# Two heads' keys per load, and the softmax's cross-partition steps on TensorE: a one-token decode block on one core

## The chip, the cores and the metric

The kernel runs on one core of a Trainium2 chip. The metric is device time in microseconds. The time before is 685.73 us, the median of 3 runs (685.69 to 685.84). The profile comes from a run of its own.

## The reference

One token passes through a transformer block: attention over a cache of 16,384 positions with 32 heads of 128 (each with keys and values of its own), then a gated feed-forward part. Six vectors from a condition `c` shift, scale and gate both parts.

```python
mod = (silu(c) @ w_mod).reshape(1, 6, 1, 640)        # sa, ca, ga, sb, cb, gb
h = layernorm(x) * (1 + ca) + sa
q = (h @ wq).reshape(32 heads, 128)
p = softmax(q . k_cache * 128 ** -0.5)               # 32 x 16384
o = p @ v_cache
x = x + ga * (o.reshape(4096) @ wo)
h = layernorm(x) * (1 + cb) + sb
x = x + gb * ((silu(h @ w_gate) * (h @ w_up)) @ w_down)
```

All tensors are bf16. Keys and values are 134.2 MB each; the weights together are 22.0 MB. Every byte is read once.

## The kernel before, in words

`build` writes a list of operations, each with an engine, a position (`pos`) and the operations that it depends on. `_Plan.emit` sorts each engine's operations by position and puts semaphore waits ahead of an operation whose dependencies are on other engines. So every engine runs a fixed order, and one that waits holds up all that stands behind it. All large loads go through SP's queue in such an order. `TK(h)` is the position at which head h's work begins.

**Start.** SP loads `w_mod` into `wreg`, `wq` into the space of the values (`vbig`), and then the keys of head 0 in four pieces and those of head 1. TensorE makes two of the six modulation vectors (`o_mod`, L330), and from them the normalised input. Eight groups of four heads (`q_ops`, L352) give the queries, broadcast to all partitions, and ScalarE copies them to `qbc` (L356). The other four modulation vectors (`o_mod_b`) come after all eight groups.

**Keys.** A head's keys lie as 128 partitions with 128 positions each, 32,768 contiguous bytes per partition (`kv`). `kring` has two such slots. VectorE multiplies the slot by the query (L434), folds the 128 products of each position to 64 (L436), to 32 and 16 (L443), and reduces these (L446) to the scores `S_sb`; L449 takes the largest per partition. The slot is then free, and SP loads the keys of the head after the next (`load_k`).

**Softmax.** GpSimd's `partition_all_reduce` takes the maximum over the partitions (L452). ScalarE scales it (L454) and makes the exponentials `P_sb` with their sum per partition (L456); GpSimd adds the sums over the partitions (L459), and ScalarE inverts them (L461, L463).

**Values.** `vring` has two slots as well, partitions and positions as the keys have them. TensorE multiplies four columns of `P_sb` with 512 columns of values, 32 times a head (L472), so the diagonal of a 4 x 4 grid of blocks holds the wanted sums. ScalarE copies the four rows out with the scaling (L484), and four small matmuls add the diagonal (L491). The value slot is free when L472's last matmul is done (`o_pvlast`); SP loads the values of the head after the next then (`load_v`). In TensorE's order, head h's product stands at `TK(h) + 28.0`, before the work of the following heads.

**End.** Heads 0 to 27 are turned to columns in groups (L515, L519), heads 28 to 31 are used as they are. The last head's values come in three pieces, each used as it lands, in matmuls of one column (L502). `wo` lies in `wreg`, and its matmuls (L560) collect the attention's output. The feed-forward weights are loaded into `kring` once the last two heads' scores are made. Then follow the second layer norm, gate and up (L624), down (L642), the sum with x (L648), a transpose and the output's store.

Of the kernel before, what the change touches and what calls it, by code (L numbers as in the profile page):

```python
# [6 lines left out]
BF16 = mybir.dt.bfloat16  # L7
# [134 lines left out]
def build(nc, A_x, A_k, A_v, A_wq, A_wo, B_wg, B_wu, B_wd, c_in, w_mod, out):  # L142
# [10 lines left out]
    GQ = 4  # L153
    PVB = 4
# [7 lines left out]
    NKP0 = 4  # L162

    def TK(h):
        return 20.0 + PERIOD * h

    es = ExitStack()
    with es:
# [3 lines left out]
        def sb(name, shape, dtype):  # L172
# [7 lines left out]
        VEX = 10240  # L180
        wreg = sb("wreg", [128, max(WM_E, H * D)], BF16)
        wm_v = wreg[:, 0:WM_E].rearrange("p (k n) -> p k n", k=KC)
        wo_v = wreg[:, 0:H * D].rearrange("p (k n) -> p k n", k=H)
        kring = sb("kring", [128, 2, TT, 128], BF16)
        vbig = sb("vbig", [128, 2 * TT * 128 + VEX], BF16)
        vring = vbig[:, 0:2 * TT * 128].rearrange("p (s t d) -> p s t d", s=2, t=TT)
        assert WQ_E - VEX <= TT * 128
        wq_v = vbig[:, 2 * TT * 128 + VEX - WQ_E:2 * TT * 128 + VEX].rearrange("p (k n) -> p k n", k=KC)
        assert FFN_E <= 2 * TT * 128
        kflat = kring[:].rearrange("p s t d -> p (s t d)")  # L190
        wg_v = kflat[:, 0:KC * F].rearrange("p (k n) -> p k n", k=KC)
        wu_v = kflat[:, KC * F:2 * KC * F].rearrange("p (k n) -> p k n", k=KC)
        wd_v = kflat[:, 2 * KC * F:2 * KC * F + FCH * D].rearrange("p (k n) -> p k n", k=FCH)
        acc_sb = sb("acc_sb", [4, 2, 512], F32)
        ident_f = sb("ident_f", [4, 4], F32)
        qbc = sb("qbc", [128, H, 128], BF16)
        S_sb = sb("S_sb", [128, 2, TT], F32)
        P_sb = sb("P_sb", [128, 2, TT], BF16)
        ones_f = sb("ones_f", [128, 128], F32)
# [10 lines left out]
        c_one = acc_sb[0:1, 0].bitcast(BF16)[:, 0:D]  # L210
        x_one = acc_sb[0:1, 1].bitcast(BF16)[:, 0:D]
        pm = sb("pm", [128, H], F32)
        gm = sb("gm", [128, H], F32)
        nb = sb("nb", [128, H], F32)
        rs = sb("rs", [128, H], F32)
        Ls = sb("Ls", [128, H], F32)
# [3 lines left out]
        warm = sb("warm", [128, 2], F32)  # L220
# [31 lines left out]
        mod_ps = psb[4]  # L252
        A_ps = psb[5]
        st_ps = psb[6]
        f_ps = psb[7]
        acc_ps = [psb[0], psb[1]]
# [3 lines left out]
        POOL, ACT, DVE, PE = "pool", "act", "dve", "pe"  # L260
# [4 lines left out]
        o_ones = op(POOL, 0.0, lambda e: e.memset(ones_bf[:], 1.0), name="ones")  # L265
        o_ident = op(POOL, 0.1, lambda e: e.affine_select(
            out=ident[:], in_=ones_bf[:], pattern=[[1, 128]], compare_op=ALU.is_equal,
            fill=0.0, base=0, channel_multiplier=-1), deps=[o_ones], name="ident")
        o_wz = op(DVE, 0.1, lambda e: e.memset(warm[:], 1.0), name="warm0")
        op(POOL, 0.2, lambda e: e.partition_all_reduce(  # L270
            warm[:, 1:2], warm[:, 0:1], channels=128, reduce_op=bass.bass_isa.ReduceOp.max), deps=[o_wz], name="warm")
# [72 lines left out]
        def q_ops(pos, g, wv, n0, ddep, h0, h1):  # L344
            n = h1 - h0
            b = g % 2
            prev = o_qev.get(g - 2)

            def f_q(e):
                last = None  # L350
                for k in range(KC):
                    last = e.matmul(q_ps[b][:, 0:n * 128], lhsT=h_col[:, k:k + 1].broadcast_to([128, 128]),  # L352
                                    rhs=wv[:, k, n0:n0 + n * 128], start=(k == 0), stop=(k == KC - 1))
                return last
            o_q[g] = op(PE, pos, f_q, deps=[ddep, o_h, prev], name="q_mm%d" % g)
            o_qev[g] = op(ACT, pos + 0.1, lambda e: e.activation(  # L356
                out=qbc[:, h0:h1].rearrange("p h d -> p (h d)"), in_=q_ps[b][:, 0:n * 128], func=ACTF.Copy),
                deps=[o_q[g]], name="qbc%d" % g)
            for h in range(h0, h1):
                o_qbc[h] = o_qev[g]  # L360

        o_qbc = [None] * H
# [5 lines left out]
        o_mod_b = op(PE, 4.5, lambda e: f_mod(e, wm_v, 2, 6, lambda o, k: slice(o + 128 * k, o + 128 * (k + 1))), deps=[d_wm, o_h], name="mod_mm_b")  # L368
        o_modc = op(ACT, 4.6, lambda e: e.activation(out=modb[:], in_=mod_ps[:, 2 * KC:6 * KC], func=ACTF.Copy), deps=[o_mod_b], name="mod_b")
        o_onep_b = op(DVE, TK(0) + 19.3, lambda e: e.tensor_scalar_add(out=onep_b[:], in0=modb[:, 2 * KC:3 * KC], scalar1=1.0), deps=[o_modc], name="onep_b")  # L370
        ga, sb_, gb = modb[:, 0:KC], modb[:, KC:2 * KC], modb[:, 3 * KC:4 * KC]
        o_gbx = op(DVE, TK(0) + 19.35, lambda e: e.tensor_copy(out=gbx, in_=gb), deps=[o_modc], name="gb_pairs")
# [3 lines left out]
        d_k = [None] * H  # L376
        d_v = [None] * H
        o_red = [None] * H
        o_exp = [None] * H
        o_pvlast = [None] * H  # L380
        o_acc = [None] * H
        o_diag = [None] * H
        o_on = [None] * H
        o_z = [None] * H
        TL = TK(H - 1)
        VSPLIT = [0, TT // 2, 3 * TT // 4, TT]

        def load_k(h):
            s2 = h % 2
            deps = [o_red[h - 2]] if h >= 2 else []  # L390
            if h == 0:
                KP = TT // NKP0
                d_k[0] = [plan.dma(0.2 + 0.01 * c, kring[:, 0, c * KP:(c + 1) * KP, :], kv(A_k, 0)[:, c * KP:(c + 1) * KP, :],
                                   ("k0", c), name="dma_k0_%d" % c) for c in range(NKP0)]
                return
            d_k[h] = [plan.dma(TK(h - 1) + 8.8 if h > 1 else 0.3, kring[:, s2], kv(A_k, h), ("k", s2), deps=deps, name="dma_k%d" % h)]

        def load_v(h, pos):
            s2 = h % 2
            cuts = VSPLIT if h == H - 1 else [0, TT]  # L400
            deps = [o_pvlast[h - 2]] if h >= 2 else o_q_all
            d_v[h] = [plan.dma(pos + 0.01 * c, vring[:, s2, a:b, :], kv(A_v, h)[:, a:b, :],
                               ("v", s2, c), deps=deps, name="dma_v%d_%d" % (h, c)) for c, (a, b) in enumerate(zip(cuts, cuts[1:]))]

        load_k(0)
        load_k(1)

        o_idf = op(ACT, 4.7, lambda e: e.activation(out=ident_f[:], in_=ident[0:4, 0:4], func=ACTF.Copy), deps=[o_ident], name="ident_f")
        o_msk, o_e8 = {}, {}
        for n in msk:  # L410
            o_msk[n] = op(DVE, TK(0) + 19.0, lambda e, n=n: e.tensor_reduce(  # L411
# [5 lines left out]
            o_e8[n] = op(DVE, TK(0) + 19.05, f_e8, deps=[o_ident], name="e%d" % n)  # L417
        o_as = [None] * len(GROUPS)

        for h in range(H):  # L420
            base = TK(h)
            s2 = h % 2
            if h + 1 < H and h >= 1:
                load_k(h + 1)
            load_v(h, base + 8.9 + (0.5 if h == H - 1 else 0.0))

            kslot = kring[:, s2]
            npc = len(d_k[h])
            KP = TT // npc
            fd = []  # L430
            for c in range(npc):
                ksl = kslot[:, c * KP:(c + 1) * KP, :]
                qb = qbc[:, h].unsqueeze(1).broadcast_to([128, KP, 128])
                o_m = op(DVE, base + 3.3 * c, lambda e, ksl=ksl, qb=qb: e.tensor_tensor(out=ksl, in0=ksl, in1=qb, op=ALU.mult),  # L434
                         deps=[d_k[h][c], o_qbc[h]], name="mult%d_%d" % (h, c))
                fd.append(op(DVE, base + 3.3 * c + 2.2 + (6.6 if npc == 1 else 0.0), lambda e, ksl=ksl: e.tensor_tensor(  # L436
                    out=ksl[:, :, 0:64], in0=ksl[:, :, 0:64], in1=ksl[:, :, 64:128], op=ALU.add),
                    deps=[o_m], name="fold1_%d_%d" % (h, c)))
            prev = fd
            w = 64  # L440
            for i in range(2):
                w //= 2
                prev = [op(DVE, base + 15.5 + 1.5 * i, lambda e, kslot=kslot, w=w: e.tensor_tensor(  # L443
                    out=kslot[:, :, 0:w], in0=kslot[:, :, 0:w], in1=kslot[:, :, w:2 * w], op=ALU.add),
                    deps=prev, name="fold%d_%d" % (i + 2, h))]
            o_red[h] = op(DVE, base + 18.2, lambda e, s2=s2, kslot=kslot, w=w: e.tensor_reduce(  # L446
                out=S_sb[:, s2], in_=kslot[:, :, 0:w], axis=AX.X, op=ALU.add),
                deps=prev + [o_exp[h - 2] if h >= 2 else None], name="red%d" % h)
            o_max = op(DVE, base + 18.5, lambda e, h=h, s2=s2: e.tensor_reduce(  # L449
                out=pm[:, h:h + 1], in_=S_sb[:, s2], axis=AX.X, op=ALU.max), deps=[o_red[h]], name="max%d" % h)  # L450

            o_gm = op(POOL, base + 19.0, lambda e, h=h: e.partition_all_reduce(  # L452
                gm[:, h:h + 1], pm[:, h:h + 1], channels=128, reduce_op=bass.bass_isa.ReduceOp.max), deps=[o_max], name="gm%d" % h)
# [13 lines left out]
            if h < H - 1:  # L467


                def f_pv(e, s2=s2):  # L470
# [6 lines left out]
                    with e.Fori(0, (TT - 16) // (4 * PVB)) as i:  # L477
                        for u in range(PVB):
                            one(i * (4 * PVB) + (8 + 4 * u), i * (512 * PVB) + (v0 + 1024 + 512 * u))
# [224 lines left out]
```

## Time and profile before

| | |
|---|---|
| Median of 3 runs | 685.73 us |
| Profiled run, its time | 685.91 us |
| Its span, from the first to the last instruction | 684.2 us |
| PE busy (matmul) | 354.2 us, 52% |
| DVE busy | 617.6 us, 90% |
| ACT busy | 79.6 us, 12% |
| POOL busy | 375.4 us, 55% |
| Mean granted TensorE clock | 0.729 |
| Read from memory | 290.48 MB, 425 GB/s over the span |

PE is TensorE, DVE is VectorE, ACT is ScalarE, POOL is GpSimd and SP is SyncE, which here only issues loads. A line of the profile names a line of the kernel (L434), an engine, an operation, and what it writes and reads. In a timeline each row has its start and its busy time in us, and in square brackets the idle time of the engine just before it and what ended that. The chain of waits is followed back from the last instruction, at each step to whatever released it. The shares of the DMA's time are shares of the core's 16 DMA engines.

### The profile page before, as it was taken

The numbers are of one execution on the slowest core, as the hardware profiler recorded it, in microseconds if no ns is written. First come the engines' busy times: TensorE is split into PE (matmuls) and PEld (weight loads), VectorE is DVE, ScalarE is ACT, GpSimd is POOL, SyncE is SP. The second block draws the span as 40 slices with busy tenths as digits, with TensorE's granted clock in tenths as the row PEclk, the third lists the DMA queues.
The fourth block names the chain that finished last, engine by engine and source line by source line (L and its number), as shares of the span: only waits on it lengthen the run. The fifth ranks groups of instructions, "written<-read, shape, count | busy, mean of one in ns | idle before, by whom it ended". The sixth has DMA issues, their size and how long they took to land.

```text
span 684.2 us, 6292 instructions
## 1 busy us (share of the span) xinstructions
PE 354.2 (52%) x1952; PEld 151.5 (22%) x1952; DVE 617.6 (90%) x228; ACT 79.6 (12%) x280; POOL 375.4 (55%) x71
## 2 busy tenths in 40 slices
PE   2345244556544544656554444655545446555565
PEld 2122012222211212222121212222112112221254
DVE  0299999999999999999999999999999999999911
ACT  1021011011101111111011111111011110110010
POOL 0005765655567766655567756655573666555700
PEclk9977676776777776676677777677767776777665
DMA  9999999999999999999999999999999999999996
GB/s 379 410 438 429 433 434 433 430 431 435 435 428 429 431 429 429 433 435 431 432 437 430 433 428 431 431 428 431 431 433 433 433 435 432 429 429 433 410 413 270
DMA packets 13689, 290.70 MB, mean 425 GB/s; under 512 B 1318, under 2 KB 2024, under 8 KB 4200
## 3 DMA queue, kind: packets, MB, share of 16 engines
q1 hardware_dynamic: 13668, 290.48, 99.2%
q8 instruction: 10, 0.16, 0.1%
q14 instruction: 7, 0.06, 0.0%
q10 hardware_dynamic: 4, 0.00, 0.0%
HBM read 290.48 MB, written 0.00 MB: 425 GB/s over the span
## 4 chain that ended last, share of the span: by engine, by line
DVE 79%; DMA 17%; SPq 3%; issue 1%; PE 0%; ACT 0%; DVEq 0%
DVE kring L434 35%; DVE kring L436 18%; DVE kring L443 14%; DMA kring<-in_A_k_cache_dram 12%; DVE S_sb L446 9%; DMA vbig<-in_A_wq_dram 4%; SPq L71 3%; DMA kring<-in_B_w_down_dram 2%; DVE pm L449 1%; PE psb L352 0%; PE psb L642 0%; ACT qbc L356 0%; DVE e L416 0%; DVE msk L411 0%; PE psb L652 0%
## 5 line engine op out<-in xcount | busy, mean ns | idle before, releaser
L472 PE MATMUL psb<-vbig,P_sb 128*4 128x512 bf16 (+1 forms) x992 | 285.7, 459 | 266.8 <-ACT P_sb L456 193.1
L452 POOL PARTITION_ALL_REDUCE gm<-pm x32 | 254.7, 7960 | 226.6 <-DVE pm L449 226.6
L434 DVE TENSOR_TENSOR kring<-kring,qbc 128x16384 bf16<-128x16384 bf16 (+1 forms) x35 | 278.4, 7953 | 14.6 <-ACT qbc L356 13.4
L472 PEld LDWEIGHTS psb<-vbig,P_sb 128*4 128x4 bf16 (+1 forms) x992 | 94.7, 98 | 444.7 <-ACT P_sb L456 237.2
L436 DVE TENSOR_TENSOR kring<-kring 128x8192 bf16<-128x8192 bf16 (+1 forms) x35 | 142.1, 4059 | 1.2
L459 POOL PARTITION_ALL_REDUCE Ls<-rs x32 | 119.6, 3738 | 32.7 <-ACT P_sb L456 32.7
L443 DVE TENSOR_TENSOR kring<-kring 128x4096 bf16<-128x4096 bf16 x64 | 112.5, 1758 | 2.2
L446 DVE TENSOR_REDUCE S_sb<-kring 128x128 f32<-128x2048 bf16 x32 | 73.2, 2286 | 1.1
L491 PE MATMUL psb<-ident_f,acc_sb 4*128 4x1 f32 x248 | 32.5, 248 | 23.8 <-ACT acc_sb L484 23.8
L484 ACT ACTIVATE acc_sb<-psb,rl 4x512 f32<-4x512 f32 x31 | 21.0, 679 | 165.3 <-PE psb L472 165.3
L491 PEld LDWEIGHTS psb<-ident_f,acc_sb 4*128 4x128 f32 x248 | 29.9, 186 | 39.5 <-ACT acc_sb L484 39.5
L454 ACT ACTIVATE nb<-gm 128x1 f32<-128x1 f32 x32 | 6.5, 202 | 214.3 <-POOL gm L452 214.3
L461 ACT ACTIVATE lnl<-Ls 128x1 f32<-128x1 f32 x32 | 6.5, 203 | 123.6 <-POOL Ls L459 123.6
L352 PE MATMUL psb<-vbig,h_col 128*128 128x512 bf16 x40 | 11.8, 468 | 10.7 <-DMA vbig<-in_A_wq_dram 10.7
L599 DVE TENSOR_TENSOR tt<-attn_bf,modb 128x5 f32<-128x5 bf16 x1 | 0.2, 167 | 14.3 <-ACT attn_bf L598 14.3
L456 ACT ACTIVATE P_sb<-S_sb,nb 128x128 bf16<-128x128 f32 x32 | 12.9, 402 | 1.2
L449 DVE TENSOR_REDUCE pm<-S_sb 128x1 f32<-128x128 f32 x32 | 9.2, 286 | 1.1
L515 ACT ACTIVATE Z<-msk,on_f 128x16 bf16<-128x16 f32 (+1 forms) x28 | 8.7, 310 | 0.9
L512 ACT ACTIVATE on_f<-psb 128x1 f32<-128x1 f32 x28 | 4.8, 171 | 31.8 <-PE psb L491 30.7
L352 PEld LDWEIGHTS psb<-vbig,h_col 128*128 128x128 bf16 x40 | 4.6, 117 | 17.5 <-DMA vbig<-in_A_wq_dram 10.8
L356 ACT ACTIVATE qbc<-psb 128x512 bf16<-128x512 f32 x8 | 4.8, 597 | 25.0 <-PE psb L352 25.0
L330 PE MATMUL psb<-silu_c,wreg 128*128 128x1 bf16 x150 | 4.8, 168 | 5.0 <-DMA wreg<-in_w_mod_dram 5.0
(75 smaller groups left out, 67.1 us busy)
## 6 DMA issues: line engine op xcount, KB each, us to landing
kring<-in_A_k_cache_dram SPq DMA_DIRECT2D x31, 4096.0 KB, 18.3
vbig<-in_A_v_cache_dram SPq DMA_DIRECT2D x31, 4096.0 KB, 27.4
vbig<-in_A_wq_dram SPq DMA_DIRECT2D x1, 5120.0 KB, 26.7
wreg<-in_w_mod_dram SPq DMA_DIRECT2D x1, 4800.0 KB, 14.2
kring<-in_A_k_cache_dram SPq DMA_DIRECT2D x4, 1024.0 KB, 31.7
wreg<-in_A_wo_dram SPq DMA_DIRECT2D x1, 3840.0 KB, 37.9
kring<-in_B_w_gate_dram SPq DMA_DIRECT2D x1, 2160.0 KB, 18.4
kring<-in_B_w_up_dram SPq DMA_DIRECT2D x1, 2160.0 KB, 23.4
```

The costliest lines, as they stand in the source:

```text
L71: return e.dma_start(out_ap, in_ap)
L352: last = e.matmul(q_ps[b][:, 0:n * 128], lhsT=h_col[:, k:k + 1].broadcast_to([128, 128]), rhs=wv[:, k, n0:n0 + n * 128], start=(k == 0), s ...
L434: o_m = op(DVE, base + 3.3 * c, lambda e, ksl=ksl, qb=qb: e.tensor_tensor(out=ksl, in0=ksl, in1=qb, op=ALU.mult), deps=[d_k[h][c], o_qbc[h ...
L436: fd.append(op(DVE, base + 3.3 * c + 2.2 + (6.6 if npc == 1 else 0.0), lambda e, ksl=ksl: e.tensor_tensor(out=ksl[:, :, 0:64], in0=ksl[:, ...
L443: prev = [op(DVE, base + 15.5 + 1.5 * i, lambda e, kslot=kslot, w=w: e.tensor_tensor(out=kslot[:, :, 0:w], in0=kslot[:, :, 0:w], in1=kslot ...
L446: o_red[h] = op(DVE, base + 18.2, lambda e, s2=s2, kslot=kslot, w=w: e.tensor_reduce(out=S_sb[:, s2], in_=kslot[:, :, 0:w], axis=AX.X, op= ...
L449: o_max = op(DVE, base + 18.5, lambda e, h=h, s2=s2: e.tensor_reduce(out=pm[:, h:h + 1], in_=S_sb[:, s2], axis=AX.X, op=ALU.max), deps=[o_ ...
L452: o_gm = op(POOL, base + 19.0, lambda e, h=h: e.partition_all_reduce(gm[:, h:h + 1], pm[:, h:h + 1], channels=128, reduce_op=bass.bass_isa ...
L459: o_L = op(POOL, base + 20.0, lambda e, h=h: e.partition_all_reduce(Ls[:, h:h + 1], rs[:, h:h + 1], channels=128, reduce_op=bass.bass_isa. ...
L472: return e.matmul(acc_ps[s2][0:4, :], lhsT=P_sb[:, s2, bass.ds(t, 4)], rhs=vbig[:, bass.ds(at, 512)], start=start, stop=stop)
L484: o_acc[h] = op(ACT, base + 28.6, lambda e, h=h, s2=s2: e.activation(out=acc_sb[:, s2], in_=acc_ps[s2][0:4, :], func=ACTF.Copy, scale=rl[0 ...
L491: last = e.matmul(OT_ps[:, h:h + 1], lhsT=acc_sb[:, s2, 128 * i:128 * (i + 1)], rhs=ident_f[:, i:i + 1], start=(i == 0), stop=(i == 3))
```

## The change

Keys are loaded two heads at a time. A unit is a pair of heads (units 0 to 14, heads 0 to 29) or a single one (units 15 and 16, heads 30 and 31). In a pair, partitions 0 to 63 hold one head and 64 to 127 the other, with 256 positions each, 65,536 contiguous bytes per partition. `kbig` has two slots of that size. `wreg` and the extra room for `wq` are gone: `w_mod` first lies in slot 1 of `kbig`, `wo` goes to slot 0 at the end, the feed-forward weights to slot 1, and `wq` fits in the values' slots. So pair 1's keys wait for all six modulation vectors, and `o_mod_b` moves up between the first two groups of queries.

GpSimd is not used any more. The largest score per partition is turned to a row by a matmul with the identity, VectorE takes the maximum of each half of that row (`top`), and a matmul with ones brings it back to the partitions. A pair's exponentials are in the keys' layout, and four matmuls with shifted identities (`place`) bring them to the values' layout, from which ScalarE copies them to `P_sb`. Sums over the partitions are a matmul with ones, for four heads at once. The scaling by the sums is taken from ScalarE's copy to VectorE, four heads at once. Masks and identities are made on VectorE at the start.

The first piece of a unit's mult is followed by the softmax of the unit before. Pair 0 comes in two pieces of 4 MB.

```diff
+    def BU(u):
+        return 20.0 + PERIOD * UNITS[u][0]
+    def EU(u):
+        return BU(u) + 18.6 * UNITS[u][1]
...
+        def load_k(u, pos, deps, cuts):
+            h, m = UNITS[u]
+            src = A_k[0, h:h + m].rearrange("h (p t) d -> (h p) t d", p=128 // m)
...
+        load_k(0, 0.2, [], [0, TT, T2])
+        load_k(1, 10.0, [o_mod, o_mod_b], [0, T2])
...
+        def stage_top(u, pos_dve):
+            o_T = op(PE, E + 0.1, lambda e: e.matmul(row_ps, lhsT=pm[:, u:u + 1], rhs=ident_f[:], start=True, stop=True),
...
+            o_sm = op(DVE, pos_dve, lambda e: e.tensor_reduce(
+                out=gm2[:, 0:m], in_=row_ps.rearrange("p (h k) -> p h k", h=m), axis=AX.X, op=ALU.max),
...
+            pt = max(E + 0.3, pos_dve + 0.01)
+            o_top[u] = op(PE, pt, f_top, deps=[o_sm, o_onesf], name="top_all%d" % u)
+            o_nb[u] = op(ACT, pt + 0.1, lambda e: e.activation(out=nb[:, u:u + 1], in_=top_ps, func=ACTF.Copy, scale=-SCALE),
...
+        for u, (h, m) in enumerate(UNITS):
+            cuts = [0, TT, T2] if u == 0 else [0, 64, nt]
...
+                if c == 0 and u:
+                    pt = softmax(u - 1, B + 4.0)
+                    hp, mp = UNITS[u - 1]
+                    if u - 1 < NU:
+                        value(hp, pt + 0.5)
+                        if hp % GQ == GQ - 2:
+                            sums(hp // GQ, pt + 0.6, hp - 2, GQ)
+                        value(hp + 1, pt + 0.7)
+                        if hp % GQ == GQ - 2:
+                            diag(hp // GQ, pt + 0.8, hp - 2, GQ)
+                    else:
+                        sums(H, pt + 0.4, hp - 2, 3)
...
+            if u < NU:
+                load_v(h, B + 8.0)
+                load_v(h + 1, B + 8.1 if u < NU - 1 else B + 8.2)
+                if u + 2 < NU:
+                    load_k(u + 2, E - 3.5, [o_red[u]], [0, T2])
...
+        pt = softmax(NU + 1, EU(NU + 1) + 0.2)
+        load_v(H - 2, BU(NU) + 6.0)
+        sums(H + 1, pt + 0.3, H - 1, 1)
+        value(H - 2, pt + 0.5)
+        diag(H // GQ - 1, pt + 0.8, HD, H - 1 - HD)
...
+        load_v(H - 1, BU(NU) + 6.2)
...
-        TO = TL + 9.0
+        TO = BU(NU) + 6.05
+        wo_free = [o_red[NU - 1]]
```

Here `NU` is 15, `TT` 128, `T2` 256, `H` 32, `HD` 28 and `GQ` 4; `value` is the product with a head's values and the copy of its four rows, and `diag` adds the diagonal blocks of up to four heads. `TL` is the position at which the last unit begins.

## The prediction

> **What bounds the kernel now.** First view: the page's DMA rows. A slice is 17.1 us.
>
> ```profile
> DMA  9999999999999999999999999999999999999996
> GB/s 379 410 438 429 433 434 433 430 431 435 435 428 429 431 429 429 433 435 431 432 437 430 433 428 431 431 428 431 431 433 433 433 435 432 429 429 433 410 413 270
> q1 hardware_dynamic: 13668, 290.48, 99.2%
> ```
>
> SP's queue keeps the 16 DMA engines full from 1.8 to 679.9 us; nothing idles until the weights of the last block are in. The chain of waits names DVE for 79% of the span; in order of time it shows why both are true:
>
> ```profile
> 476.45 8.61 DVE kring L434
> 485.08 4.44 DVE kring L436
> 489.54 2.30 DVE kring L443
> 495.44 20.50 DMA kring<-in_A_k_cache_dram
> 515.96 8.70 DVE kring L434
> ...
> 612.77 19.74 DMA kring<-in_A_k_cache_dram
> 632.54 8.70 DVE kring L434
> ```
>
> Up to 495 us the mults (L434) follow each other at 19.28 us a head, DVE's own sum. From then on every other mult waits for its keys, and two heads take 38.86 us, 19.43 each: the DMA's pace. The packets of the trace agree: a head's 4 MB is 8 packets of 32,768 B per engine at 1.218 us, 9.74, and K plus V are 19.5. So DVE is 1% faster than the DMA and its early lead of a few us is used up at 495. The third view is the timeline's tail:
>
> ```profile
> 642.38 10.02 PE L472 MATMUL psb<-vbig,P_sb 128*4 128x512 bf16 x32 [8.12 <-DMA vbig<-in_A_v_cache_dram]
> 651.62 0.29 DVE L449 TENSOR_REDUCE pm<-S_sb 128x1 f32<-128x128 f32 x1
> 652.43 0.68 ACT L484 ACTIVATE acc_sb<-psb,rl 4x512 f32<-4x512 f32 x1 [6.03 <-PE psb L472]
> 653.16 1.05 PE L491 MATMUL psb<-ident_f,acc_sb 4*128 4x1 f32 x8 [0.77 <-ACT acc_sb L484]
> 654.14 3.82 PE L560 MATMUL psb<-A_sb,wreg 128*128 128x1 bf16 x140
> 666.74 0.26 ACT L524 ACTIVATE On<-psb,rl 128x1 bf16<-128x1 f32 x1 [10.76 <-PE psb L502]
> 670.82 2.25 PE L624 MATMUL psb<-h_col,kring 128*128 128x1 bf16 x70 [1.04 <-DVE h_col L608]
> 675.46 2.25 PE L624 MATMUL psb<-h_col,kring 128*128 128x1 bf16 x70 [2.39 <-DMA kring<-in_B_w_up_dram]
> 680.99 0.79 PE L642 MATMUL psb<-gu_col,kring 128*128 128x1 bf16 x20 [0.63 <-DMA kring<-in_B_w_down_dram]
> 681.81 0.18 DVE L648 TENSOR_TENSOR_SCAN o_pair<-psb,gx 128x10 bf16<-128x10 f32 x1 [3.82 <-PE psb L642]
> ```
>
> The last maximum is done at T0 = 651.9. Head 30's value product (L472, the first line) had run beside DVE's work and was ready at 652.4. After that PE has slack: "up" and "down" wait for DMA, and the end at 684.2 is the last weight plus some 3 us. The profiled run took 685.91, 1.72 over its span; the median is 685.73. A change under 0.2% (1.4 us) can't be told from none.
>
> **The change, part by part.**
>
> *Bytes and packets.* No byte goes. The new size is 65,536 B per partition for 14 pair loads, 8 rows per engine each, 112 in all. No packet of it is in the trace. Upper row: as two packets of 32,768 B, 2,436 ns, no gain. Lower: packets of 38,400 and 40,960 B (each one packet) took 1,420 and 1,514 ns, 27.2 B per ns, so one of 65,536 is 1,218 + 1,205 = 2,423 ns, 13 saved, 1.5 us over 112. On the other side, cut into 8,192 B (309 ns each) a row takes 2,472, 4 us lost. The row of 40,960 B is nearest: it went whole. I take half of 1.5, as a cut in two is as simple. Rows of 64 KB also double the distance between what neighbouring engines read.
>
> The Trainium skill (DMA: Bandwidth & Descriptors, "Latency and other measured facts") says that a row pitch at a large power of two slows HBM copies, 207 GB/s at 512 KiB against a full 214, and it speaks against this change. By it, as an estimate, the pairs could lose 3%, 9 us in all, and the sum would be some 9 us longer.
>
> In this trace the keys' rows at a power-of-two pitch (32 KiB) run at 26.9 B per ns and the 40,960 B rows, whose pitch is none, at 27.1, so the doubling is taken as free.
>
> *DVE, start.* Pair 0 comes in two pieces of 4 MB where head 0 came in four of 1 MB. The first lands at 26.6 (wq's last data) + 9.75 + 1.44 = 37.8. (1.44 is checked on head 31: 62 loads of 4 MB before and with it, 26.6 + 604.5 + 1.44 = 632.5, its mult's start.) Mults start at 37.8, not 31.0. The rows of 2,048, 4,096, 8,192 and 16,384 elements (1.224, 2.291, 4.425, 8.684 us) make 0.157 us + 0.521 ns per element. Pair 0: 2 x (8.68 + 4.43) + 4.43 + 2.29 + 4.42 (reduce, twice 2.286 less its fixed part) + 0.42 + gaps = 38.0, end at 75.8.
>
> *DVE, each pair after.* 4.43 + 12.96 (mult in 64 and 192 rows) + 8.69 + 4.43 + 2.29 + 4.42 + 0.42, a row reduce of 0.29 ("top", nearest the max's 0.286), half an "on" of 0.17, gaps: 38.15, against 38.57. "top" waits for a PE transpose some 1 us long, covered by the first mult piece (4.43); without that cover 14 us would be lost. The saving hides: the DMA needs 39.0 a pair. Keys of pair 14 land after 56 loads, 26.6 + 546 + 1.44 = 574.0 (572.5 with whole rows); DVE alone would want them at 75.8 + 13 x 38.15 = 571.8. Then 38.15 + two single units of 19.8 give T0 = 650.3 to 651.8. I take 651.0, 0.9 before today's.
>
> *Queues.* Pair 1's load waits for the second modulation block (moved between query groups, 2.64 us, done at 33), and V0 queues behind it on SP; K0 keeps the DMA busy to 46. V30 waits for product 28, done near 628.7, while V29 lasts to 631; wo and V31 stand behind it on SP. A gap up to 1 us is possible, and is not on the new path. Later weights queue behind V31 as before.
>
> *GpSimd.* Both all-reduces (254.7 and 119.6 us busy) go; their 8 us waits lay beside DVE's mults, and alone they took 0.35 and 0.39. A shorter softmax mid-run only lets values start sooner; DMA order is full anyway. DVE gains nothing: its duration fits one line with and without POOL busy. PE gets some 3 us of small work a pair and ACT 5 (transpose, broadcast, placing, copies), in 39 of which products take 18: hidden.
>
> *The tail, where it costs.* In the new order on PE, product 30 stands at pt + 0.5 behind the last unit's "row", "top_all" and sum, each waiting on T0. V30 is in by 643 and exp30 by 638, but PE, in order, idles. After T0: row, top, broadcast, nb, exp, sum = 0.65 + 0.34 + 0.65 + 0.25 + 0.65 + 0.65 = 3.2 (f32 matmuls of two records at 0.59, ACT at 0.20 and 0.40 + 0.19; 2.4 to 3.9); product 30 at the mean of 31, 9.2 (8.5 to 10.0, by when the clock goes from 0.5 to 1.0); acc 0.75; diag 1.1; wo 3.85 + 0.5; product 31 in L502's pieces 3.7; from it to gate 4.1 (666.70 to 670.82); gate and up 2.25 each, now without a wait; gu 0.35; down 2.3; rest 2.4. Sum 35.95, against 32.3 from T0 today. Down starts at T0 + 31.3 = 682.3, so all weights are in. Span 651.0 + 35.95 = 687.0, time 688.7, on the median's scale 688.5: 2.8 slower. Bounds: 650.3 + 33.6 and 651.8 + 37.5, which is 685.4 to 690.8.
>
> **Rivals.**
> 1. *The DMA keeps setting the end, no change* (0.16): PE's tail is shorter than summed, 685 to 687. For it: product 30 may take 8.5, and matvecs 27 ns instead of 32 if the clock stays up behind it (gate, up, down 0.9 less). Against: three low ends have to meet.
> 2. *Faster* (0.07): whole 65,536 B packets save 1.5 us and fewer loads 0.3, and the last weight still decides: 683.9. It decides when PE reaches "down" before 679.2, 29 us after T0 = 650.3; my sum has 31.3.
> 3. *The doubled rows read slower* (0.07): the keys set the pace and T0 moves with them. At the price of 8,192 B pieces the keys land 4 us after the packets in two, T0 is 655.8 and the end 693. It decides as soon as a row of 64 KB takes over 2,436 ns. For it: no such row in the trace. Against: the 40,960 B rows.
>
> **How the numbers follow.** The forecast (PE's serial tail) has 0.70: 688.5, own range 686.4 to 690.8. It gives slower at 0.9 of its chance; rival 3 adds 0.07, rival 1 a little. Slower 0.73, same 0.19, faster 0.08. The range for 8 in 10 reaches down into rival 1 and up to the forecast's end: 685.4 to 691.5.
>
> **What would show it.** Right: DMA still 9 in all slices but the last two; a product of 32 matmuls starting some 3 us after the last maximum; "up" following "gate" without a wait for w_up; no wait of "down" for DMA; T0 at 650 to 652; pair period near 39.0 late in the run. Wrong: product 30 ended before T0, "down" waiting for weights, or key packets of 65,536 B much over 2,436 ns.

## The result and the profile after

| | before | after |
|---|---|---|
| Median | 685.73 us (685.67 to 685.84, 5 runs) | 692.85 us (692.08 to 693.48, 5 runs) |
| Profiled run, its span | 685.91, 684.2 | 692.85, 691.1 |
| POOL busy | 375.4 us | 0.2 us |
| DVE busy | 617.6 us | 612.9 us |

The ratio is 1.0103 (95% interval 1.0088 to 1.0117): 1.0% slower, 7.1 us. The direction was forecast; the size was not, and 692.85 lies above the range's end of 691.5.

The page's DMA rows of the changed kernel:

```profile
DMA  9999999999999999999999999999999999999991
GB/s 394 417 442 425 436 439 425 458 403 448 421 436 424 465 408 427 451 421 432 424 438 434 450 408 429 453 419 439 421 459 412 450 413 435 430 427 417 417 415 64
q1 hardware_dynamic: 11220, 290.48, 97.9%
```

The engines are as full as before, with the same bytes in fewer packets, and they are done earlier: the last slice moves 64 GB/s where it moved 270. By the packets of the trace the last weight is in at 677.6 us (680.5 before, where the prediction has 679.9). So the loads cost nothing, and the end is 13 us behind them. The chain of waits, in order of time (start, length, what), goes through VectorE's mults up to 270 us and from then on mostly through the values' loads, which SP issues behind the products. At the end it reads:

```profile
599.12 30.49 DMA vbig<-in_A_v_cache_dram
629.65 8.86 PE psb L529 x32
639.05 4.34 DVE kbig L577
...
653.78 0.30 DVE pm L601
654.12 0.60 PE psb L464 x2
...
657.02 9.22 PE psb L529 x32
666.27 0.59 ACT acc_sb L540
666.91 1.05 PE psb L547 x8
667.96 4.10 PE psb L670 x155
672.07 0.51 PE psb L631 x19
672.57 2.17 issue
674.74 3.06 PE psb L631 x109
...
681.81 4.44 PE psb L733 x140
686.57 2.13 PE psb L751 x70
```

From 654 us on all of it is TensorE's work, one piece behind another: the row of maxima (L464), product 30 (L529), the diagonal (L547), `wo` (L670), product 31 (L631), gate and up (L733), down (L751). That is the forecast's tail. Two things in it were not forecast. One is the first rows: VectorE's work of the last unit follows on a TensorE product at 629.65 to 638.5. The timeline there:

```profile
625.74 0.59 ACT L540 ACTIVATE acc_sb<-psb 4x512 f32<-4x512 f32 x1 [8.95 <-PE psb L529]
628.53 0.29 DVE L601 TENSOR_REDUCE pm<-S_sb 128x1 f32<-128x128 f32 x1
628.74 4.42 DVE L577 TENSOR_TENSOR kbig<-kbig,qbc 128x8192 bf16<-128x8192 bf16 x1
629.65 8.86 PE L529 MATMUL psb<-vbig,P_sb 128*4 128x512 bf16 x32 [3.94 <-DMA vbig<-in_A_v_cache_dram]
638.35 0.38 PE L464 MATMUL psb<-ident_f,pm 128*1 128x128 f32 x2
638.77 0.28 DVE L466 TENSOR_REDUCE gm<-psb 1x1 f32<-1x128 f32 x1 [5.61 <-PE psb L464]
```

Product 28 ends before 625.74. Unit 15's maximum is there at 628.8, but its row (L464) stands behind product 29 on TensorE, which waits for its values until 629.65 and runs to 638.5. VectorE does the first mult piece of unit 16 and then stands for 5.61 us before it can take the maximum of that row. T0, the end of the last maximum, is 654.07. The other thing is the idle 2.17 us that the chain calls "issue", inside product 31.

### The profile page after: what moved, and what is told of

Same layout as the page of the kernel before. It is cut to its first block, busy times and chain, and to the rows that moved or that the text cites. A ratio compares the mean times of both kernels' runs of the same rounds, so it can differ in the third digit from the quotient of the medians.

```text
span 691.1 us, 5975 instructions
## 1 busy us (share of the span) xinstructions
PE 330.8 (48%) x1946; PEld 137.7 (20%) x1946; DVE 612.9 (89%) x195; ACT 66.3 (10%) x210; POOL 0.2 (0%) x4
## 4 chain that ended last, share of the span: by engine, by line
DMA 42%; DVE 36%; PE 20%; issue 1%; ACT 1%; SPq 0%; DVEq 0%
DMA vbig<-in_A_v_cache_dram 33%; PE psb L529 16%; DVE kbig L577 16%; DVE kbig L597 13%; DMA kbig<-in_A_k_cache_dram 5%; DMA x_row<-in_A_x_dram 4%; DVE S_sb L599 4%; DVE kbig L592 1%; PE psb L733 1%; PE psb L670 1%; PE psb L631 1%; ACT P_k L492 0%; PE psb L751 0%; DVE pm L601 0%; DVE gm L466 0%
## 5 line engine op out<-in xcount | busy, mean ns | idle before, releaser
L577 DVE TENSOR_TENSOR kbig<-kbig,qbc 128x8192 bf16<-128x8192 bf16 (+2 forms) x34 | 278.0, 8175 | 23.8 <-DMA kbig<-in_A_k_cache_dram 23.8
L529 PE MATMUL psb<-vbig,P_sb 128*4 128x512 bf16 (+1 forms) x992 | 258.1, 418 | 26.4 <-DMA vbig<-in_A_v_cache_dram 20.6
L597 DVE TENSOR_TENSOR kbig<-kbig 128x8192 bf16<-128x8192 bf16 (+3 forms) x50 | 238.3, 4766 | 1.7
L529 PEld LDWEIGHTS psb<-vbig,P_sb 128*4 128x4 bf16 (+1 forms) x992 | 88.2, 89 | 189.1 <-issue 85.3
L464 PE MATMUL psb<-ident_f,pm 128*1 128x128 f32 x34 | 9.6, 381 | 199.5 <-DVE pm L601 199.5
L599 DVE TENSOR_REDUCE S_sb<-kbig 128x256 f32<-128x4096 bf16 (+1 forms) x17 | 70.9, 4169 | 0.6
L540 ACT ACTIVATE acc_sb<-psb 4x512 f32<-4x512 f32 x31 | 18.2, 586 | 268.3 <-PE psb L529 268.3
L464 PEld LDWEIGHTS psb<-ident_f,pm 128*1 128x1 f32 x34 | 1.5, 81 | 204.5 <-DVE pm L601 204.2
L504 PE MATMUL psb<-P_k,place 128*128 128x128 bf16 x60 | 9.1, 308 | 22.9 <-ACT P_k L492 22.9
L492 ACT ACTIVATE P_k<-S_sb,nb 64x256 bf16<-64x256 f32 x30 | 15.2, 506 | 0.9
L547 PE MATMUL psb<-sel,acc_sb 128*128 128x4 f32 (+1 forms) x64 | 8.4, 255 | 5.4 <-ACT acc_sb L540 5.4
L547 PEld LDWEIGHTS psb<-sel,acc_sb 128*128 128x128 f32 x64 | 7.7, 191 | 9.4 <-ACT acc_sb L540 9.4
L592 DVE TENSOR_TENSOR kbig<-kbig 128x8192 bf16<-128x8192 bf16 x2 | 8.8, 4424 | 0.1
```

What stands on the lines that cost most here:

```text
L464: o_T = op(PE, E + 0.1, lambda e: e.matmul(row_ps, lhsT=pm[:, u:u + 1], rhs=ident_f[:], start=True, stop=True), deps=[o_max[u], o_idf, lnl ...
L492: o_exp[h + hh] = op(ACT, pt + 0.2 + 0.01 * hh, lambda e, p_=p_, hh=hh: e.activation(out=P_k[p_], in_=S_sb[p_, :], func=ACTF.Exp, scale=SC ...
L504: last = e.matmul(R_ps[:, TT * hh:TT * (hh + 1)], lhsT=place[:, hh, eo, :], rhs=P_k[:, TT * eo:TT * (eo + 1)], start=(eo == 0), stop=(eo = ...
L529: return e.matmul(acc_ps[s2][0:4, :], lhsT=P_sb[:, s2, bass.ds(t, 4)], rhs=vbig[:, bass.ds(at, 512)], start=start, stop=stop)
L540: o_acc[h] = op(ACT, pos + 0.05, lambda e: e.activation(out=acc_sb[32 * j:32 * j + 4], in_=acc_ps[s2][0:4, :], func=ACTF.Copy), deps=[o_pv ...
L547: last = e.matmul(OT_ps[:, h0:h0 + n], lhsT=acc_sb[:, 128 * i:128 * (i + 1)], rhs=sel[:, i, 0:n], start=(i == 0), stop=(i == 3))
```

## The experiments

Theory A: the whole loss is the order on TensorE at the end, product 30 behind the last row and unit 15's row behind product 29. Rival R: the loads are the loss, rows of 64 KB or values whose loads wait for products on SP. Rival G: GpSimd's absence matters to VectorE. The first four are compared with a median of 685.77 us for the kernel before, the last two with 685.80.

**Product 30 early.** It goes where the other products stand, ahead of the last row:

```diff
                     else:
                         sums(H, pt + 0.4, hp - 2, 3)
+                        load_v(H - 2, BU(NU) + 6.0)
+                        value(H - 2, pt + 0.5)
+                        diag(H // GQ - 1, pt + 0.8, HD, H - 1 - HD)
...
         pt = softmax(NU + 1, EU(NU + 1) + 0.2)
-        load_v(H - 2, BU(NU) + 6.0)
         sums(H + 1, pt + 0.3, H - 1, 1)
-        value(H - 2, pt + 0.5)
-        diag(H // GQ - 1, pt + 0.8, HD, H - 1 - HD)
```

> Product 30, its copy and the diagonal sums are put ahead of the last unit's row on TensorE, as in the kernel before; nothing else is moved. Theory A (TensorE's order at the end is the loss): T0, the end of the last maximum, stays at 654, product 30 runs at 640 to 650, the 9.3 us go from the tail until the last weight decides: weights in at 677 to 678, the end 4.3 us after the last packet as before, span 681.3, time 683.1. Rival R (the loss lies in the loads: rows of 64 KB and value loads that wait for products on SP): the tail only waits elsewhere, time 690 or more.

Measured: 684.28 us, ratio to before 0.9978 (0.9969 to 0.9987), 8.6 us under the changed kernel. Its timeline:

```profile
638.66 0.28 DVE L466 TENSOR_REDUCE gm<-psb 1x1 f32<-1x128 f32 x1 [5.50 <-PE psb L464]
640.48 7.80 PE L529 MATMUL psb<-vbig,P_sb 128*4 128x512 bf16 x32
653.67 0.29 DVE L604 TENSOR_REDUCE pm<-S_sb 128x1 f32<-128x128 f32 x1
679.41 0.78 PE L751 MATMUL psb<-gu_col,kbig 128*128 128x1 bf16 x20 [0.58 <-DMA kbig<-in_B_w_down_dram]
```

T0 is as late as before the edit (653.96) and VectorE still stands 5.5 us, but product 30 is done at 648.3, and the last "down" waits 0.58 us for its weights again: the DMA sets the end. R falls. The span is 682.6, 1.3 over the expected: the last packets came at 678.9 and not at 677.6. The end stands 3.7 us behind them, as it does in the kernel before; with 679.9 for the last weight it would be the expectation's 4.3.

**The row first.** Product 29 is put behind unit 15's row, and the load that waits for it (head 31's values) moves with it; product 30 stays in the tail:

```diff
-                        value(hp + 1, pt + 0.7)
+                        value(hp + 1, pt + 0.7 if u < NU else E + 0.2)
...
-        load_v(H - 1, BU(NU) + 6.2)
+        load_v(H - 1, EU(NU) + 0.3)
```

> The row of unit 15's maxima goes ahead of product 29 on TensorE; product 30 stays in the tail. Theory A: VectorE's idle 5.6 us before unit 15's top go, T0 is 648.5 instead of 654.1, and the end moves with it: span 685.5, time 687.3. Rival R: product 29 waits for its values anyway and what VectorE gains it loses at the next keys or values; time within 1 us of 692.9.

Measured: 686.73 us, ratio 1.0017 (1.0008 to 1.0026), 6.1 under the changed kernel.

```profile
628.82 0.58 PE L464 MATMUL psb<-ident_f,pm 128*1 128x128 f32 x2 [2.44 <-DVE pm L601]
629.64 8.31 PE L529 MATMUL psb<-vbig,P_sb 128*4 128x512 bf16 x32 [0.23 <-DMA vbig<-in_A_v_cache_dram]
633.02 0.27 DVE L466 TENSOR_REDUCE gm<-psb 1x1 f32<-1x128 f32 x1
648.02 0.28 DVE L601 TENSOR_REDUCE pm<-S_sb 128x1 f32<-128x128 f32 x1
651.20 9.46 PE L529 MATMUL psb<-vbig,P_sb 128*4 128x512 bf16 x32
```

The row runs in the time in which TensorE waited for values anyway, and product 29 starts at the same 629.64. VectorE's stall is gone (row 3 has no idle time), T0 is 648.30, 5.8 earlier, and the end moves with it.

**Both.**

> Both moves. Theory A: T0 648.5, but the DMA sets the end in the first move already, so no more than there: weights in at 677 to 678, span 681.3, time 683.1, below the kernel before. If instead TensorE still sets the end in the first move, this one is up to 5.6 us shorter than it. Rival R: 690 or more.

Measured: 684.35 us, ratio 0.9978 (0.9969 to 0.9987). T0 is 648.30, and the time is that of product 30 early alone. So the two faults don't add: with product 30 out of the tail a T0 that is 5.7 us later (653.96 against 648.30) costs nothing, as the weights end the run either way; with it in the tail those us of T0 count in full.

```profile
648.01 0.29 DVE L604 TENSOR_REDUCE pm<-S_sb 128x1 f32<-128x128 f32 x1
667.56 2.23 PE L733 MATMUL psb<-h_col,kbig 128*128 128x1 bf16 x70 [1.34 <-DMA kbig<-in_B_w_gate_dram]
673.90 2.25 PE L733 MATMUL psb<-h_col,kbig 128*128 128x1 bf16 x70 [4.11 <-DMA kbig<-in_B_w_up_dram]
679.40 0.79 PE L751 MATMUL psb<-gu_col,kbig 128*128 128x1 bf16 x20 [0.70 <-DMA kbig<-in_B_w_down_dram]
```

The first line ends at T0. Gate, up and down all wait for weights here.

**Both, and no packet of 65,536 B.**

```diff
-                    load_k(u + 2, E - 3.5, [o_red[u]], [0, T2])
+                    load_k(u + 2, E - 3.5, [o_red[u]], [0, TT, T2])
...
-                               deps=[d_k[u][c if u == 0 else 0], o_qbc[u]], name="mult%d_%d" % (u, c)))
+                               deps=([d_k[u][c]] if u == 0 else d_k[u]) + [o_qbc[u]], name="mult%d_%d" % (u, c)))
```

(and the same cuts for pair 1)

> Both moves, and each pair's keys in two loads of 32,768 B per partition, so that no packet of 65,536 B is left; same bytes, same slots. Theory A: the DMA sets the end, so the packets count: 13 ns for each of 112 pairs of packets per engine, 1.5 us, and some 0.1 for 14 more loads: 1.6 us longer than both moves alone, 684.7. Rival R (rows of 64 KB are the slow part): shorter than both moves alone by several us.

Measured: 685.47 us, 1.1 over both moves alone (1.6 expected), and by its ratio to before, 0.9995 (0.9986 to 1.0004), no different from the kernel before. In the trace the 1,792 packets of 65,536 B took 2,423 ns each on the mean, 271.3 us per engine; the 3,584 of 32,768 B that take their place 1,217.5, 272.7. So 12 ns a pair of packets, 1.4 us, most of it seen in the time. Without the rows of 64 KB no gain over the kernel before is left that these runs could tell from none.

**GpSimd back.** Both moves, and GpSimd's all-reduces beside the rest, into tiles that nobody reads:

```diff
+            for i in range(h, h + m):
+                op(POOL, E + 0.1 + 0.01 * (i - h), lambda e, u=u, i=i: e.partition_all_reduce(
+                    gm_d[:, i:i + 1], pm[:, u:u + 1], channels=128, reduce_op=bass.bass_isa.ReduceOp.max), deps=[o_max[u]], name="gm_d%d" % i)
```

(and one after each head's exponentials for the sum, except for head 31; so there are 63 and not the 64 that the expectation names)

> Both moves as before, and GpSimd runs its 64 all-reduces (maximum and sum) beside the rest again, into tiles that nobody reads. Theory A: GpSimd waits for VectorE's instructions and VectorE not for it, so the period of a pair stays at 37.9 us and the time at 684.35 +- 0.5; taking GpSimd out gave nothing. Rival G (GpSimd did hold VectorE up, its removal hid part of the loss): each all-reduce, 0.35 to 0.39 us alone, delays VectorE, 1.5 us a pair, T0 some 20 us later than 648, time 696 to 700.

Measured: 684.32 us. The groups of the instructions by line (busy us, mean ns), first GpSimd's, then VectorE's largest:

```profile
L583 POOL PARTITION_ALL_REDUCE Ls_d<-rs x31 | 223.9, 7271 | 31.1 <-ACT P_k L493 24.9 <-ACT P_sb L497 6.2
L611 POOL PARTITION_ALL_REDUCE gm_d<-pm x32 | 191.9, 6044 | 202.3 <-DVE pm L608 150.9 <-DVE on_f L555 51.4
L578 DVE TENSOR_TENSOR kbig<-kbig,qbc 128x24576 bf16<-128x24576 bf16 x14 | 181.1, 12936 | 0.0
```

The last row is the same as in the changed kernel, where GpSimd does nothing, to the ns:

```profile
L577 DVE TENSOR_TENSOR kbig<-kbig,qbc 128x24576 bf16<-128x24576 bf16 x14 | 181.1, 12936 | 0.0
```

415.8 us of GpSimd cost nothing: its all-reduces take 6.0 and 7.3 us on the mean, and VectorE's largest mults not a ns more. The last all-reduce, at 648.29, finds VectorE idle and takes 0.35. G falls. The Trainium skill (SBUF — State Buffer, "Who interferes with whom") says of VectorE's and GpSimd's shared port pair that whoever issues first has it and the other blocks. Here only GpSimd's side of that is seen: VectorE's mult begins first (75.76 us for pair 1, the all-reduce at 75.94).

**One fault alone in the kernel before.** Heads stay single and GpSimd works; only product 30 and what follows it wait for the last exponentials:

```diff
+        o_pvlast[H - 2].deps.append(o_exp[H - 1])
...
-                o_pvlast[h] = op(PE, base + 28.0, f_pv,
+                o_pvlast[h] = op(PE, base + 28.0 if h < H - 2 else TL + 20.65, f_pv,
```

(copy, diagonal and `on` of head 30 in the same way at TL + 20.7 to 20.9)

> The kernel before (heads one by one, GpSimd in use), with one part of the change alone: head 30's value product, its copy and its sums wait for the last head's exponentials. Theory A: the exponentials are done at T0 + 1.3 = 653.2, and from the start of product 30 to the end of the span the changed kernel and the one with the row first took 34.1 and 34.0 us: span 687.3, time 689.0, 3.3 slower than before. If the tail were hidden by the weights still being loaded: 685.8.

Measured: 690.64 us, ratio 1.0076 (1.0063 to 1.0090), 4.8 slower than before.

```profile
651.22 0.29 DVE L449 TENSOR_REDUCE pm<-S_sb 128x1 f32<-128x128 f32 x1
652.76 8.48 PE L472 MATMUL psb<-vbig,P_sb 128*4 128x512 bf16 x32 [18.62 <-ACT P_sb L456]
668.14 0.45 PE L561 MATMUL psb<-On,wreg 128*128 128x1 bf16 x11 [1.34 <-issue]
674.22 0.48 PE L502 MATMUL psb<-P_sb,vbig 128*128 128x1 bf16 x12 [1.96 <-issue]
```

With the order of one product the kernel before loses 4.8 us, where the changed one loses 7.1. That is more than the 1.0 of the row first, whose T0 is 3.2 us earlier. The expectation was 1.6 us short of the median, 0.8 of it in the profiled run (689.83 us). There the start of product 30 to the end of the span took 35.3 us against 34.1 expected, and the "issue" rows, 3.3 us together, are more than the 2.2 and 1.9 of the two kernels it was sized on.

## Why the prediction was right in direction and wrong in size

**Right: what bounds, and the mechanism.** The DMA did stay full, no byte and no DMA time was lost, and the serial tail on TensorE behind product 30 ended the run. Taking product 30 out of it put the end back on the weights, below the kernel before. Rivals 1 and 2, in which the weights set the end, did not come in the changed kernel; that end is seen only once product 30 is moved, with 684.28 for rival 2's 683.9. That one-column matmuls take 27 ns or 32, which rival 1 put down to the clock, is not the clock alone: at the same granted clock of 0.50 the last 109 one-column matmuls of product 31 took 28.0 ns each and the 140 of gate and up 31.6. Rival 3, slow rows of 64 KB, is refuted: 2,423 ns is the figure worked out for a whole packet, and the half gain taken (0.75 us) should have been a whole one (1.1 measured). The 9 us that the prediction estimated from what the Trainium skill says of row pitch (DMA: Bandwidth & Descriptors, "Latency and other measured facts") did not come: rows of 64 KB, which lie here one behind the other, ran at 27.05 B per ns, those of 32 KB at 26.9. No run here has a pitch of 512 KiB, for which the skill gives its 207 GB/s.

**The step that failed: T0, "38.15 + two single units of 19.8".** For "top" the prediction says that VectorE's wait for the transpose is covered by the first mult piece. That looked at how long the row takes (0.6 us) and not at what stands ahead of it on TensorE. In a pair there is time: 38 us between rows. In a single unit there are 19.5, and product 29, with values due at 631 by the prediction's own paragraph on queues, lies across the row. Unit 15 took 609.20 to 628.74, 19.5; from there to T0 are 25.3 instead of 19.8, with the 5.6 of VectorE's stall in them. With the stall taken away T0 was 648.30, 5.8 earlier, so the rest of that step had put T0 2.7 us too late: keys of pair 14 came at 571.3 (572.5 to 574.0), a pair took VectorE 37.9 (38.15), a single unit 19.5. T0 as a whole: 654.1 for 651.0.

**A term that was mis-sized: product 31, 3.7 us.** It took 5.9 (671.93 to 677.79), 2.17 of them "issue". The tail is 37.0 from T0, for 35.95. The other terms held: 2.9 for 3.2 up to product 30, 9.3 for 9.2, gate and up 4.4 for 4.5.

**The sum.** Span 691.1 for 687.0: 3.1 from T0 (5.8 of stall, less 2.7 of earlier work) and 1.0 from the tail. The upper bound had taken in a slow product and late keys, but no wait for an order. The forecast's cause alone, without the stall, is the run with the row first: 686.73, 1.0 slower than before and 1.8 under the 688.5.

**The signs.** All but T0 came, the late pair period among them. Pairs 11 to 14 begin at 454.97, 493.78, 532.55 and 571.32 us, each after a wait of 0.5 to 0.9 us for its keys, so the period is 38.8, set by the DMA (a pair's keys at 2,423 ns a packet and two heads' values at 1,218 make 38.9):

```profile
571.32 4.42 DVE L577 TENSOR_TENSOR kbig<-kbig,qbc 128x8192 bf16<-128x8192 bf16 x1 [0.88 <-DMA kbig<-in_A_k_cache_dram]
```

**In all.** From both moves (684.35) to the changed kernel are 8.5 us: product 30 in the tail gives 2.4 (686.73), the row behind product 29 the other 6.1 once the tail decides. Against before, the rest of the change is worth 1.4 us, of which the rows of 64 KB give 1.1.

## What to carry to other kernels

When loads are merged into larger units, write down each in-order engine's queue for the last units by itself: what had a whole unit's time between two steps has half of it where the units are cut smaller again, and a short step behind a long one that waits for data holds up whoever needs the short one. An operation with its inputs ready long before the last dependency should stand ahead of everything that waits for it. And this kernel, whose DMA is full from start to end, had 1.1 us to gain in the middle from larger packets and 8.5 to lose at the end.

## What the runs showed of the hardware that was not expected

TensorE stalls of 0.8 to 2.2 us that no semaphore explains ("issue") lie in the tail of six of the eight profiles, in the unrolled one-column matmuls; with both moves and with GpSimd back there is none. In the changed kernel the trace has a packet of 16,384 B on the queue of instructions at 672.1 and the stall from 672.6 to 674.7; with product 30 early a packet at 661.1 and the stall from 661.6 to 663.6; with the row first 666.4 and 667.0 to 668.9. All nine such stalls end 2.4 to 2.7 us after a packet of this size began. That TensorE waits for its next instructions, fetched by the same busy DMA engines, fits them all. It would also explain why the last weights came 1.3 us later with product 30 early (six packets of instructions from 600 us on, against four in the changed kernel). Neither was tried by itself.
